# Weight loads ahead of later steps' loads on SP, and results written from ScalarE's queue

## The chip, the core and the metric

One NeuronCore of a Trainium2 chip runs the whole program. The metric is the device time of one execution in microseconds (us); the median over the runs is taken. The profile adds one execution with its hardware trace.

## What is computed

Attention over four batches of 8 heads, 768 positions and head size 64. Each query sees the first four keys (the sinks) and a window of the last 128. What attention gives, 3072 rows of 512, goes through a two-layer network with 2048 hidden units. Inputs and results are float32.

```python
def _attn_ref(q, k, v, n_sink, window):
    scores = scale * np.matmul(q, k.transpose(0, 1, 3, 2))
    is_sink = pos[None, :] < int(n_sink)
    rel = pos[:, None] - pos[None, :]
    keep = is_sink | ((rel >= 0) & (rel < int(window)))
    scores = np.where(keep, scores, -1000000000.0)
    ...
    return np.matmul(a, v).astype(np.float32)

def _moe_ref(x, w_in, w_out):
    h = x @ w_in
    sp = np.maximum(h, 0.0) + np.log1p(np.exp(-np.abs(h)))
    g = h * erf(sp)
    return (g @ w_out).astype(np.float32)
```

`w_in` and `w_out` arrive as float64.

## The kernel before, in words

**Work.** The 3072 rows are cut into 12 groups of 256. A group has four attention steps, one for each pair of heads, so there are 48 steps (0 to 47). Each step loads k and q (tile `kq`) and v (tile `v`), turns them (`tqk`), multiplies (`ps`), takes the softmax on VectorE (DVE) and ScalarE (ACT), turns the weights of the softmax (`tp`, `ts` in the first steps, through `turn`, `pd`, `pa` in DRAM later) and multiplies with v (`av`). The network follows behind: for each group 16 slices of the hidden layer (`h`, lines L766 and L770), the function on ACT (L783 to L788, three `u` tiles for each pair of slices) with its products on DVE (L792), giving `gf` in the first part and `g` (L799 on DVE, L800 on GpSimd) later, then the second product into `o` (L812, later L815 to L817), then a copy `ot` (L821, ACT) and a DMA to the result (L732). Each group has two results, `ot_g_0` and `ot_g_1`, so there are 24.

**Weights.** They come in 32 blocks of 512 KB (`ws`, L653). Three DVE instructions for a block (L665, L670, L673) make float32 of float64's two halves (`wf`). While not all are there, TensorE (PE) multiplies in float32 straight from `wf` (L766, L812: the float32 stage); later ACT and DVE split them (`wt`, L684, L685) and PE runs on the split form (L770, L815 to L817). `wl` issues the next blocks, up to ten ahead of those converted.

**Sinks.** The first four rows of v are needed for each step. For later groups they are spread into a DRAM tile `sinks` once (`set_sinks`, L253): one DMA of 1024 KB from `vz` (L256) and four of 64 KB from the input (L263). From step 12 on, a group's steps read them back (L248).

**Order.** The Tile framework's scheduler writes out each engine's order from priorities: `with at(a, what)` gives the place of what is issued there, `plan` says which step does what at which place. `follow(prev, ins)` (L330) only says that `ins` stands behind `prev` in that order; nothing waits on it. SP issues nearly all DMAs, one after another. A DMA that is issued waits on its engine for its data, for its buffer, and on one of eight semaphores (`DMAHW0` to `DMAHW7`) for the landing of an earlier DMA, the one issued eight before it as a rule. Results share their buffers (tag `u`, four of them) with the `u` tiles.

The lines that the change touches: L225 and L241 (kq and v in `load`, L209), L256 in `set_sinks`, L653 in `wload`, L732. Numbers behind names (`ws_394`, `gf_713`) count tiles as they are made; `kq_890` and `v_932` are those of step 8, `v_1090` of step 9, `v_1221` of step 10, and `ws_186` is the ninth weight block.

Of the kernel before, what the change touches and what calls it, by code (L numbers as in the profile page):

```python
# [9 lines left out]
F32 = mybir.dt.float32  # L10
BF16 = mybir.dt.bfloat16
F32R = mybir.dt.float32r
I32 = mybir.dt.int32
# [6 lines left out]
P = 128  # L20
# [42 lines left out]
def kernel(  # L63
# [11 lines left out]
    nc = tc.nc  # L75
    B, H, S, D = q.shape
    NT, DM = out.shape
# [60 lines left out]
    def fast_path():  # L138
        with ExitStack() as st:
# [20 lines left out]
                out=kw[:, :256], in0=rf[:, :256], scalar=0.0, in1=kw[:, :256], op0=ALU.is_ge, op1=ALU.mult  # L160
# [42 lines left out]
            mark = {}  # L203
# [5 lines left out]
            def load(s, what="kq"):  # L209
                g, c = divmod(s, NPAIR)  # L210
                b, gb = divmod(g, GPB)
                d = stp.setdefault(s, {})
                if "k" in what:
                    t = d["kq"] = raw.tile([P, 2, GT], F32, tag="kq", bufs=1, name=f"kq_{s}")
                    if s < DT:
                        d["k"], d["q"] = (t[:, j].rearrange("p (n h d) -> p n h d", n=2, h=2) for j in range(2))
                if "k" in what or "q" in what:
                    t = d["kq"]
                    last = mark.get(("d", s - 2))
                    for j, src in enumerate((k, q)):  # L220
                        if "kq"[j] not in what:
                            continue
                        for h in range(2):
                            if s < DT:
                                nc.sync.dma_start(  # L225
                                    d["kq"[j]][:, :, h, :],
                                    src[b, 2 * c + h, gb * GT : (gb + 1) * GT, :].rearrange("(n p) d -> p n d", p=P),
                                )
                                continue
                            for e in range(2):  # L230
                                p0 = 64 * h + 32 * e
                                x = nc.sync.dma_start(
                                    t[p0 : p0 + 32, j, :].rearrange("p (n c) -> p n c", c=32),
                                    src[b, 2 * c + h, gb * GT : (gb + 1) * GT, 32 * e : 32 * e + 32].rearrange("(n r) c -> r n c", r=32),
                                )
                                last = mark["l", s] = follow(last, x)
                if "v" in what:
                    t = d["v"] = raw.tile([P, 3, 2, D], F32, tag="v", bufs=1 + AL, name=f"v_{s}")
                    m0 = 0 if gb == 0 else 1
                    for h in range(2):  # L240
                        x = nc.sync.dma_start(  # L241
                            t[:, 1 - m0 :, h, :],
                            v[b, 2 * c + h, gb * GT - m0 * P : (gb + 1) * GT, :].rearrange("(n p) d -> p n d", p=P),
                        )
                        follow(mark.get(("r", s - 2), mark.get(("l", s))), x)
                if gb == 0 and "v" in what:
                    for z, hf in enumerate((hi, lo)):
                        nc.sync.dma_start(  # L248
                            vz[hf, z, :, 2 * c : 2 * c + 2].rearrange("p i h d -> p i (h d)"),
                            sinks[b * NPAIR + c].rearrange("p i h d -> p i (h d)"),  # L250
                        )

            def set_sinks():  # L253

                x = vz[HP : HP + 2 * SW, 0, 1].rearrange("p h d -> p (h d)").rearrange("p (o f) -> p o f", o=1)
                nc.sync.dma_start(  # L256
                    sinks.rearrange("n p i h d -> (n p i h d)").rearrange("(p o f) -> p o f", p=2 * SW, f=H * D),
                    x.broadcast_to([2 * SW, B * NPAIR, H * D]),
                )
                for i in range(2):  # L260
                    for h in range(2):
                        r0 = 2 * SW * i + SW * h
                        nc.sync.dma_start(  # L263
                            sinks[:, r0 : r0 + SW, i, h],
                            v.rearrange("b (c h) s d -> h (b c) s d", h=2)[h, :, :SW, :],
                        )
# [63 lines left out]
            def follow(prev, ins):  # L330

                if prev is not None:
                    tc.add_manual_dep(
                        ins.ins, prev.ins.name,
                        mybir.DependencyInfo(mybir.DependencyClass.NoSync, mybir.DependencyReason.DATA), reason="order",
                    )
                return ins
# [246 lines left out]
            def at(a, what):  # L584

                key = int(a * PW) + O[what] + (E.get(what, 0) if a < EA else 0)
                return tc.high_priority(offset=tc.tile_snap_priority() + 1 - key)

            def pos(s):

                return s if s < NE else 3 * s - 6 if s < 2 * NPAIR else 4 * s - 12

            plan = {}
            for s in range(NSTEP + AL):
# [23 lines left out]
                if s < 2 * NPAIR:  # L618
                    x = pos(s) + (3 if s < NE else 5)
# [9 lines left out]
            def attn(a):  # L629

                for what, fn, s in sorted(plan.get(a, ()), key=lambda x: (STAGES.index(x[0]), x[2])):
                    with at(a, "prepl" if what == "prep" and s > TT else what):
                        fn(s)
# [3 lines left out]
            def need(n):  # L637
                return 4 * (n // 4) if n < 16 else n - 16 + LAG
# [3 lines left out]
            for n in range(32):  # L642
                x = n - 16
                split.setdefault(NF - 5 + n if x < 0 else NF + 6 + (x - FH) * 5 // 4 if x >= FH else 2 * NF - 1 + x * 2 // 3, []).append(n)

            def wload(n):

                src = wblock(n)
                t = staged[n] = wpool.tile([P, 2 * DM], I32, tag="wo", name=f"ws_{n}")
                if src.dtype == F32:  # L650
                    nc.sync.dma_start(t[:, :DM].bitcast(F32), src)
                else:
                    nc.sync.dma_start(t, src.bitcast(I32))  # L653

            def wconv(n, wn):

# [30 lines left out]
            def wblock(n):  # L687
                if n < 16:
                    j, c = divmod(n, NC)
                    return w_in[c * P : (c + 1) * P, WB * j : WB * j + WB]  # L690
                return w_out[(n - 16) * P : (n - 15) * P, :]

            mlp = make_mlp(work, ps_h, ps_o)
# [18 lines left out]
            for m in range(-LEAD, NG * NF + LAG + 2):  # L712
                a = m + LEAD
                live = 0 <= m < NG * NF
                if live:
                    g, f = divmod(m, NF)
                    if f % 2 == 0:
                        hp = mlp.hid_tile(m)
                    if f > 0:
                        with at(a, "hid"):  # L720
                            ahead = mlp.hidden(hp, xp[g], f)
                attn(a)
                w = m - LAG
                if 0 <= w < NG * NF:
                    g2, f2 = divmod(w, NF)
                    with at(a, "proj"):
                        mlp.project(gs[w // 2], g2, f2, lambda ins: follow(ahead if live and f and g >= 2 else None, ins))
                    if f2 == NF - 1:
                        for i in range(2):
                            r0 = (g2 * 2 + i) * P  # L730
                            with at(a, "res"):
                                nc.sync.dma_start(out[r0 : r0 + P, :], mlp.result(g2, i))  # L732
                if live:
                    if f == 0:
                        with at(a, "hid"):
                            mlp.hidden(hp, xp[g], f)
                    if f % 2 == 1:
                        with at(a, "act"):
                            gs[m // 2] = mlp.act(hp, m, m < NF + FH)

                while wn < 32 and a >= 1 and (wn < (0, 0, 3, 5)[a - 1] if a < 5 else wn < 2 * a - 4 or need(order[wn]) <= m + W1):
                    with at(a, "wc"):
                        wconv(order[wn], wn)
                    wn += 1
                    with at(a, "wl"):
                        for n in order[wl : wn + WQ]:
                            wload(n)
                            wl += 1
                for n in split.get(m, ()):
                    with at(a, "ws"):  # L750
                        wsplit(n, m)
# [72 lines left out]
    def general_path():  # L824

        NT_S = S // P
        with ExitStack() as st:
# [71 lines left out]
            with tc.tile_pool(name="g_one1", bufs=1) as one, tc.tile_pool(name="g_work1", bufs=2) as work:  # L899
# [3 lines left out]
                with tc.For_i(0, B, 1) as b:  # L903
                    for gb in range(GPB):
# [25 lines left out]
                        for i in range(2):  # L930
# [3 lines left out]
                            )  # L934

    fast_path()
    ok = nc.values_load(flagi[0:1, 0:1], min_val=0, max_val=1)
    with tc.If(ok == 0):
# [31 lines left out]
```

## Time and profile before

| what | before |
|---|---|
| median of 3 runs | 718.12 us (716.73 to 719.35) |
| the profiled execution | 719.41 us |
| its span in the trace | 717.4 us |
| mean granted clock of PE | 0.993 |
| busy: PE, DVE, ACT, GpSimd (POOL) | 96%, 77%, 69%, 42% |

The span is what the trace covers; 2.0 us of the profiled execution lie outside it. Busy times are shares of the span; the clock is the share of full speed that was granted to PE.

### The profile page before, as it was taken

How to read it: one execution, taken by the hardware profiler on the slowest of the kernel's cores; microseconds unless marked ns; L12 is line 12 of the kernel's file. 1: busy time of each engine (PE TensorE's matmuls, PEld its weight loads, DVE VectorE, ACT ScalarE, POOL GpSimd, SP SyncE). 2: the span in 40 equal slices, each digit the busy share in tenths (PEclk: the TensorE clock that was granted, in tenths of full speed). 3: DMA queues.
4: the chain of work that ended last, by engine and by line, in shares of the span. 5: the costliest groups of instructions: out<-in, count | busy, mean ns of one | idle time of the engine just before them, and what ended most of it. 6: DMA issues, size and time to landing. Idle time of an engine off the chain costs nothing. (4 is left out here: it accounts for less than half of the span.)

```text
span 717.4 us, 16155 instructions
## 1 busy us (share of the span) xinstructions
PE 689.5 (96%) x5515; PEld 568.2 (79%) x5515; DVE 549.4 (77%) x1473; ACT 493.6 (69%) x1157; POOL 299.1 (42%) x501
## 2 busy tenths in 40 slices
PE   6779999999999999999999999999999999999997
PEld 3566557688887888788788888888888888889885
DVE  6979997687789888788888588688698687754352
ACT  4777676986984867476677586586677577586572
POOL 3412400234444546454554444555554437342221
PEclk9999999999999999999999999999999999999999
DMA  6999410302216454543553363463463543220001
GB/s 159 283 320 344 168 27 5 78 16 46 66 34 118 102 117 100 127 104 72 124 118 72 65 135 74 87 136 75 95 124 72 102 96 71 44 68 1 30 1 35
DMA packets 246858, 70.10 MB, mean 98 GB/s; under 512 B 214704, under 2 KB 238896, under 8 KB 246768
## 3 DMA queue, kind: packets, MB, share of 16 engines
q1 hardware_dynamic: 246208, 68.92, 41.1%
q8 instruction: 46, 0.75, 0.4%
q14 instruction: 44, 0.36, 0.2%
q10 hardware_dynamic: 560, 0.07, 0.1%
HBM read 50.27 MB, written 18.42 MB: 96 GB/s over the span
## 5 line engine op out<-in xcount | busy, mean ns | idle before, releaser
L770 PE MATMUL h<-xh,wt 128*128 128x256 f32 x1408 | 275.1, 284 | 0.8 <-DVE u L792 0.7
L770 PEld LDWEIGHTS h<-xh,wt 128*128 128x128 f32 x1408 | 223.7, 188 | 15.4 <-issue 8.2
L770 PE MATMUL h<-xl,wt 128*128 128x256 f32 x704 | 197.3, 281 | 0.0
L800 POOL TENSOR_TENSOR g<-u,g 128x512 fp32r<-128x512 f32 x84 | 113.9, 1356 | 181.3 <-DVE g L799 160.1
L788 ACT ACTIVATE u<-r 128x512 f32<-128x512 f32 x288 | 163.1, 622 | 19.2 <-DMA out_dram<-ot 5.3
L792 DVE SCALAR_TENSOR_TENSOR u<-u,u 128x512 f32<-128x512 f32 x168 | 136.6, 813 | 14.0 <-ACT u L788 1.6
L770 PEld LDWEIGHTS h<-xl,wt 128*128 128x128 f32 x704 | 132.1, 188 | 7.0 <-issue 2.8
L815 PE MATMUL o<-wt,g 128*128 128x512 f32 x336 | 134.1, 399 | 0.5 <-DVE g L799 0.5
L816 PE MATMUL o<-wt,g 128*128 128x512 f32 x336 | 132.8, 395 | 0.0
L817 PE MATMUL o<-wt,g 128*128 128x512 f32 x336 | 129.8, 397 | 0.6 <-POOL g L800 0.4
L426 ACT ACTIVATE pst<-pst,neg 128x144 f32<-128x144 f32 x192 | 77.4, 405 | 61.0 <-DVE neg L422 60.7
L792 DVE SCALAR_TENSOR_TENSOR u<-u,h 128x512 f32<-128x512 f32 x84 | 56.8, 676 | 54.9 <-ACT u L788 53.1
L783 ACT ACTIVATE r<-h 128x512 f32<-128x512 f32 x96 | 56.8, 592 | 51.0 <-PE h L770 42.8
L522 POOL TENSOR_SCALAR_AFFINE_SELECT pz<-pa 64x256 f32<-64x256 f32 (+1 forms) x96 | 47.1, 491 | 70.0 <-ACT pa L484 68.9
L815 PEld LDWEIGHTS o<-wt,g 128*128 128x128 f32 x336 | 63.0, 187 | 14.6 <-ACT u L788 1.3
L817 PEld LDWEIGHTS o<-wt,g 128*128 128x128 f32 x336 | 61.7, 187 | 16.0 <-POOL g L800 1.4
L816 PEld LDWEIGHTS o<-wt,g 128*128 128x128 f32 x336 | 63.0, 188 | 10.8 <-issue 0.3
L785 ACT ACTIVATE r<-r 128x512 f32<-128x512 f32 x96 | 60.6, 631 | 2.8
L784 ACT ACTIVATE r<-r 128x512 f32<-128x512 f32 x96 | 60.6, 631 | 2.6
L799 DVE CAST g<-u 128x512 fp32r<-128x512 f32 x84 | 37.4, 445 | 27.3 <-PE o L817 24.1
L513 POOL COPY pz<-pa 64x256 f32<-64x256 f32 x66 | 31.5, 477 | 55.4 <-DMA pa<-pd 54.6
L522 POOL TENSOR_SCALAR_AFFINE_SELECT pa<-pa 64x256 f32<-64x256 f32 (+1 forms) x96 | 50.4, 525 | 4.9
(99 smaller groups left out, 916.6 us busy)
## 6 DMA issues: line engine op xcount, KB each, us to landing
pd<-turn SPq DMA_DIRECT2D x33, 320.0 KB, 2.6
pa<-pd SPq DMA_DIRECT2D x132, 80.0 KB, 2.6
ws<-in_moe_w_in_dram SPq DMA_DIRECT2D x16, 512.0 KB, 6.1
ws<-in_moe_w_out_dram SPq DMA_DIRECT2D x16, 512.0 KB, 8.5
out_dram<-ot SPq DMA_DIRECT2D x24, 256.0 KB, 2.4
v<-in_v_dram SPq DMA_DIRECT2D x56, 96.0 KB, 2.5
kq<-in_k_dram SPq DMA_DIRECT2D x144, 32.0 KB, 2.0
kq<-in_q_dram SPq DMA_DIRECT2D x144, 32.0 KB, 2.2
```

The source lines that it names most:

```text
L426: mark["e", s] = nc.scalar.activation(y, y, AF.Exp, bias=d["neg"][:, i, h : h + 1], scale=-1.0, accum_out=d["sum"][:, i, h : h + 1])
L522: nc.gpsimd.affine_select(out=out, in_=x, pattern=[[0, 2], [0, 2 - i0], [-sg, HP]], compare_op=op, fill=0.0, base=0, channel_multiplier=sg,)
L770: last = nc.tensor.matmul(o, wt[NC * j + c][:, p, fs], xt[e][:, c, :], start=(m == 0), stop=(m == len(ops) - 1))
L783: nc.scalar.activation(r, h, AF.Tanh, bias=b_t, scale=0.5)
L784: nc.scalar.activation(r, r, AF.Square, bias=b_v, scale=-0.5)
L785: nc.scalar.activation(r, r, AF.Square, bias=b_r)
L788: sq = nc.scalar.activation(u, r, AF.Square, bias=b_a[i], scale=CS)
L792: pr = nc.vector.scalar_tensor_tensor(out=acc, in0=u, scalar=CC[i] * CS**2, in1=x, op0=ALU.add, op1=ALU.mult)
L800: nc.gpsimd.tensor_tensor(gl, acc, gh.bitcast(F32), op=ALU.subtract)
L815: behind(nc.tensor.matmul(o, gh[:, ws], wt[16 + f][:, 0, :], start=(f == 0), stop=False))
L816: nc.tensor.matmul(o, gh[:, ws], wt[16 + f][:, 1, :], start=False, stop=False)
L817: nc.tensor.matmul(o, gl[:, ws], wt[16 + f][:, 0, :], start=False, stop=(f == NF - 1))
```

## The change

kq and v loads of steps that are issued once a weight DMA is on record, and the sinks' spreading, are put behind the last weight DMA that is on record at that point of the program. Results are issued on ACT's queue.

```diff
@@ load @@
-                                nc.sync.dma_start(
+                                x = nc.sync.dma_start(
...
+                                follow(mark["w"], x)
...
-                        follow(mark.get(("r", s - 2), mark.get(("l", s))), x)
+                        follow(mark.get(("r", s - 2), mark.get(("l", s), mark["w"])), x)
@@ set_sinks @@
-                nc.sync.dma_start(
+                x = nc.sync.dma_start(
                     sinks.rearrange("n p i h d -> (n p i h d)").rearrange("(p o f) -> p o f", p=2 * SW, f=H * D),
                     x.broadcast_to([2 * SW, B * NPAIR, H * D]),
                 )
+                follow(mark["w"], x)
@@ wload @@
-                    nc.sync.dma_start(t, src.bitcast(I32))
+                    mark["w"] = nc.sync.dma_start(t, src.bitcast(I32))
@@ results @@
-                                nc.sync.dma_start(out[r0 : r0 + P, :], mlp.result(g2, i))
+                                nc.scalar.dma_start(out[r0 : r0 + P, :], mlp.result(g2, i))
```

Line numbers of the changed kernel are up to two higher. Three places of the order that it sets:

**SP behind the ninth weight block.** Before, with `ws_394` the tenth block:

```order
L653 DMA ws_186<-in_moe_w_out_dram 128x1024
L937 TENSOR_LOAD flagi
L937 ISA x2
L241 DMA v_932<-in_v_dram 128x3x64 x2
L241 DMA v_1090<-in_v_dram 128x3x64 x2
L256 DMA sinks<-vz 512x1x512
L653 DMA ws_394<-in_moe_w_out_dram 128x1024
L653 DMA ws_396<-in_moe_w_out_dram 128x1024
L653 DMA ws_401<-in_moe_w_out_dram 128x1024
L241 DMA v_1221<-in_v_dram 128x3x64 x2
```

The same queue in the changed kernel, from the last weight block on (`ws_814`):

```order
L655 DMA ws_814<-in_moe_w_out_dram 128x1024
L225 DMA kq_890<-in_k_dram 128x2x64 x2
L225 DMA kq_890<-in_q_dram 128x2x64 x2
L242 DMA v_932<-in_v_dram 128x3x64 x2
L242 DMA v_1090<-in_v_dram 128x3x64 x2
L257 DMA sinks<-vz 512x1x512
L242 DMA v_1221<-in_v_dram 128x3x64 x2
L265 DMA sinks<-in_v_dram 16x16x64 x4
```

The v loads of steps 8 to 10, the kq loads of step 8 and the five DMAs of the spreading stood between weight blocks, and now stand behind all of them.

**DVE at the tenth weight block.** Before, from the last work ahead of it to the first product of `gf_713`:

```order
L665 TENSOR_SCALAR wf_579<-ws_186 128x512
L673 SCALAR_TENSOR_TENSOR wf_558<-ws_181,wf_558 128x512
L670 SCALAR_TENSOR_TENSOR wf_579<-ws_186,wf_579 128x512
L433 TENSOR_SCALAR sum_537<-sum_537 128x4
L673 SCALAR_TENSOR_TENSOR wf_579<-ws_186,wf_579 128x512
L434 RECIPROCAL sum_537<-sum_537 128x4
L456 TENSOR_TENSOR snk_576<-pst,sum_537 128x128
L665 TENSOR_SCALAR wf_579<-ws_394 128x512
L670 SCALAR_TENSOR_TENSOR wf_579<-ws_394,wf_579 128x512
L417 COPY_PREDICATED ps_622<-tri,ps_622 64x2x2x64
L792 SCALAR_TENSOR_TENSOR gf_713<-u_1_717,h_652 128x512
```

Changed, from that block's first conversion (which now stands two instructions behind `ws_186`'s) on:

```order
L667 TENSOR_SCALAR wf_579<-ws_394 128x512
L672 SCALAR_TENSOR_TENSOR wf_579<-ws_186,wf_579 128x512
L435 TENSOR_SCALAR sum_537<-sum_537 128x4
L672 SCALAR_TENSOR_TENSOR wf_579<-ws_394,wf_579 128x512
L675 SCALAR_TENSOR_TENSOR wf_579<-ws_186,wf_579 128x512
L667 TENSOR_SCALAR wf_609<-ws_396 128x512
L436 RECIPROCAL sum_537<-sum_537 128x4
L675 SCALAR_TENSOR_TENSOR wf_579<-ws_394,wf_579 128x512
L667 TENSOR_SCALAR wf_609<-ws_401 128x512
L672 SCALAR_TENSOR_TENSOR wf_609<-ws_396,wf_609 128x512
L458 TENSOR_TENSOR snk_576<-pst,sum_537 128x128
L794 SCALAR_TENSOR_TENSOR gf_713<-u_1_717,h_652 128x512
```

The conversions of the tenth block, and half of those of the two after it, moved ahead of the softmax's `snk_576` and of `gf_713`.

**ACT at the results of group 5**, with what each instruction waits for. Before:

```order
L821 COPY ot_0_5200<-o_0_4502 128x512 [waits PE_49]
L821 COPY ot_1_5203<-o_1_4503 128x512 [waits PE_49]
L788 ACTIVATE u_99_5210<-r_5206 128x512 [waits Activation_49,Pool_49]
L788 ACTIVATE u_99_5213<-r_5206 128x512 [waits Pool_49]
L581 CAST xh_5169<-av_5488 128x256 [waits PE_49]
L788 ACTIVATE u_99_5216<-r_5206 128x512 [waits DMAHW5_49,Activation_49]
```

Changed:

```order
L823 COPY ot_0_5200<-o_0_4502 128x512 [waits PE_49,Pool_49]
L734 DMA out_dram<-ot_0_5200 128x512 [waits DMAHW7_49,Activation_49]
L823 COPY ot_1_5203<-o_1_4503 128x512 [waits PE_49]
L790 ACTIVATE u_99_5210<-r_5206 128x512
L790 ACTIVATE u_99_5213<-r_5206 128x512 [waits Pool_49]
L583 CAST xh_5169<-av_5488 128x256 [waits PE_49]
L734 DMA out_dram<-ot_1_5203 128x512 [waits DMAHW2_49,Activation_49]
L790 ACTIVATE u_99_5216<-r_5206 128x512 [waits DMAHW7_49]
```

Each result's DMA now stands in ACT's order, and waits there for an earlier DMA's landing as well as for its copy. At the first of them `DMAHW7` stands for the landing of the first q load of step 33, which SP issues; at the last `u` it stands for the first result's own landing.

## Rows read from the trace of the kernel before

**Rows 1.** The page's first part: busy us, share of the span, instructions.
```profile
PE 689.5 (96%) x5515; PEld 568.2 (79%) x5515; DVE 549.4 (77%) x1473; ACT 493.6 (69%) x1157; POOL 299.1 (42%) x501
```

**Rows 2.** Waits of PE: total us, times, longest us.
```profile
PE av L563 <- POOL pa L522: 6.5, 5, 2.8
```

**Rows 3.** Stretches: us; busy PE, PEld, DVE, ACT, POOL; PEclk, DMA share, GB/s.
```profile
36.00:54.00 18.00, 14.06 (x97) 10.67 (x97) 13.45 (x40) 13.66 (x38) 3.01 (x6) 0.91 1.01 320
48.00:53.00 5.00, 5.00 (x16) 3.95 (x15) 4.91 (x16) 3.84 (x12) 1.34 (x2) 0.66 1.04 406
54.00:72.00 18.00, 18.00 (x107) 12.10 (x104) 17.84 (x46) 12.75 (x33) 5.21 (x6) 1.00 1.04 344
72.00:90.00 18.00, 16.82 (x110) 10.72 (x108) 17.91 (x42) 12.17 (x31) 8.76 (x13) 1.00 0.41 163
97.00:126.00 29.00, 29.00 (x174) 18.83 (x173) 23.95 (x64) 18.16 (x45) 1.66 (x4) 1.00 0.05 10
```

**Rows 4.** Timeline of PE: start us, us, what [idle before <-releaser].
```profile
47.84 5.38 PE L766 MATMUL h<-xf,wf 128*128 128x256 f32 x16 [3.47 <-DVE gf L792]
...
57.60 3.62 PE L766 MATMUL h<-xf,wf 128*128 128x256 f32 x16
...
85.75 0.70 PE L766 MATMUL h<-xf,wf 128*128 128x256 f32 x2 [0.87 <-DVE wf L673]
86.68 2.43 PE L766 MATMUL h<-xf,wf 128*128 128x256 f32 x10 [0.24 <-DVE wf L673]
```

**Rows 5.** Timeline of DVE around the tenth weight block.
```profile
38.44 0.42 DVE L665 TENSOR_SCALAR wf<-ws 128x512 int32<-128x512 int32 x1
...
45.50 0.43 DVE L665 TENSOR_SCALAR wf<-ws 128x512 int32<-128x512 int32 x1 [4.29 <-DMA ws<-in_moe_w_out_dram]
...
47.02 0.67 DVE L792 SCALAR_TENSOR_TENSOR gf<-u,h 128x512 f32<-128x512 f32 x1
```

**Rows 6.** Timeline of SP: DMAs issued behind the ninth weight block, and the last weights.
```profile
34.53 1.99 SPq L241 DMA_DIRECT2D v<-in_v_dram  x4
36.56 0.70 SPq L256 DMA_DIRECT2D sinks<-vz  x1
37.31 4.93 SPq L653 DMA_DIRECT2D ws<-in_moe_w_out_dram  x3
...
64.20 5.94 SPq L653 DMA_DIRECT2D ws<-in_moe_w_out_dram  x8
```

**Rows 7.** DMAs issued from 30 to 92 us: KB each, us to landing.
```profile
sinks<-vz SPq DMA_DIRECT2D x1, 1024.0 KB, 7.5
```

**Rows 8.** Waits of SP on the results' copies: total us, times, longest us.
```profile
SPq L732 <- ACT ot L821: 108.5, 10, 41.3
```

**Rows 9.** ACT's timeline at the start: one of three DMAs that it issues.
```profile
1.28 0.45 ACTq L293 DMA_DIRECT2D q_early<-in_q_dram  x1
```

**Rows 10.** ACT's timeline at the results of group 5.
```profile
410.84 1.29 ACT L821 COPY ot<-o 128x512 f32<-128x512 f32 x2 [0.72 <-PE o L817]
...
413.94 0.63 ACT L788 ACTIVATE u<-r 128x512 f32<-128x512 f32 x1 [0.50 <-DMA out_dram<-ot]
```

**Rows 11.** SP's timeline there.
```profile
413.36 2.33 SPq L232 DMA_DIRECT2D kq<-in_q_dram  x4
```

**Rows 12.** The page's last part, DMA issues: KB each, median us to landing.
```profile
out_dram<-ot SPq DMA_DIRECT2D x24, 256.0 KB, 2.4
...
kq<-in_q_dram SPq DMA_DIRECT2D x144, 32.0 KB, 2.2
```

**Rows 13.** DVE's timeline there: the cast of that step's product.
```profile
416.05 0.43 DVE L799 CAST g<-u 128x512 fp32r<-128x512 f32 x1
```

**Rows 14.** PE's timeline there: the first matmul that reads it.
```profile
419.15 0.40 PE L815 MATMUL o<-wt,g 128*128 128x512 f32 x1
```

**Rows 15.** ACT's timeline at the end: the last two copies.
```profile
711.73 1.23 ACT L821 COPY ot<-o 128x512 f32<-128x512 f32 x2 [4.81 <-PE o L817]
```

More of the change, by code (lines that the diff above doesn't have):

```diff
@@ L650, in wload @@
                 if src.dtype == F32:
-                    nc.sync.dma_start(t[:, :DM].bitcast(F32), src)
+                    mark["w"] = nc.sync.dma_start(t[:, :DM].bitcast(F32), src)
                 else:
-                    nc.sync.dma_start(t, src.bitcast(I32))
+                    mark["w"] = nc.sync.dma_start(t, src.bitcast(I32))
             def wconv(n, wn):
```

## The prediction

> **What bounds the kernel now.** I began with the page's busy times: TensorE works 96% of the span [rows 1], so the end moves only by what PE loses in idle time or at a lower clock. PE's list of waits names no large one that repeats; the longest kind is for GpSimd's `pa`, 6.5 us in five waits of at most 2.8 [rows 2]. So the question is which single losses the change touches, and the stretches tell where to look. From 36 to 54 us PE is busy 14.06 of 18 us, at 0.91 of the clock, while DMA is at 1.01 of its engines [rows 3]. Here the loads are the limit. From 54 to 90 us DVE is busy 17.84 and 17.91 of 18 [rows 3]: there the conversion of weights is the limit. After that neither is full: from 97 to 126 us PE is busy 29.00 of 29, DVE 23.95, DMA at 0.05.
>
> The timelines name the loss. DVE stands 4.29 us until 45.50 for the tenth weight block [rows 5]. Behind that conversion stands the first product of `gf` at 47.02, and PE stands 3.47 us for it, until 47.84 [rows 4, 5]. Then PE is slower still: sixteen matmuls take 5.38 us where the same sixteen take 3.62 at 57.60 [rows 4], and the granted clock from 48 to 53 us is 0.66 on average [rows 3], so part of it ran at 1.2 GHz in place of 2.4 after the idle time. Two more waits, 0.87 and 0.24 us, are for conversions at 85.75 and 86.68 [rows 4].
>
> **Part one: the loads.** Before the tenth block SP issues four v loads and the 1024 KB spreading [rows 6]. They hold 4 times 96 KB and 1024 KB, 1.41 MB; at the 320 GB/s of that stretch [rows 3] that is 4.4 us, and the spreading alone needs 7.5 us from issue to landing [rows 7]. Without them in front the tenth block lands at least 4.4 us earlier than 45.50, at 41.1 or before, and DVE has work until then: its last instruction before the wait ends 4.29 us ahead of 45.50, at 41.2. So I take the whole wait as gone. The later blocks gain more, since the v of step 10, the kq of step 8 and the four small spreading loads leave too; DMA stays ahead of DVE, which needs about 1.7 us for a block (0.43 for L665 [rows 5], some 0.6 for each of the other two, an estimate from the spacing of rows in that timeline).
>
> What does PE get? Its losses in this stretch are 3.47 of idle time, 5.38 less 3.62, which is 1.76, of clock, and 0.87 with 0.24, which is 1.11, of later waits: 6.34 in all [rows 4]. But DVE is full from 54 to 90 us, and PE waits for its conversions again near 86, so up to there PE cannot come further ahead than DVE does: 4.29. The bounds are 2.4 (3.47 of idle time without the clock, and 1.11 of waits for conversions once more) and 6.3. I take **4.3**, since the full rows of DVE make that the limit. The clock comes back in this as part of the 4.3: without the 3.47 us of idle time before it I expect full speed in those sixteen matmuls.
>
> The moved loads get late themselves. The last weights are issued from 64.20 to 70.1 [rows 6]; the change lets them end earlier and puts kq of step 8, v of steps 8 to 10 and the spreading behind. In the changed order PE turns step 8's kq behind more of the float32 stage's products than before, so nothing waits where it waited before. What is later on PE is the attention of steps 7 and 8, in the stretch from 97 to 126 us; PE has no idle time there and DVE has 5 of 29 us free [rows 3]. Price: **0**, at most 2.8, the longest wait that PE has for the attention's other parts [rows 2], and not below zero, as PE is full there.
>
> **Part two: the results.** 24 DMAs leave SP for ACT. ACT's own issues at the start take 0.45 us [rows 9], so 24 of them are 10.8 us of ACT, which is busy 69% [rows 1]; PE does not wait for ACT in most places, so this alone costs nothing. Its cover is ACT's free 31%; where that is gone the waits are priced next. SP loses the waits for the copies, 108.5 us in ten [rows 8]; no wait of PE is laid to SP's results, so I count no gain.
>
> The new cost is that a result's DMA waits on ACT for an earlier DMA's landing, with the `u` activations behind it. At group 5 the two copies run 410.84 to 412.13, so the first ends near 411.43 [rows 10]. In the order that the change sets, its DMA waits for the first q load of step 33, which SP issues at 413.36 [rows 11] and which lands 2.2 us later [rows 12], 415.6. Without results SP comes there a little sooner, say 415.4. ACT stands about 4 us. The result lands 2.4 us after its issue [rows 12], at 417.8, and the third `u`, which waits for that landing, starts then and not at 413.94 [rows 10]: 3.9 us later. The cast of that step's product moves from an end of 416.48 [rows 13] to 420.4, and PE wants it at 419.15 [rows 14]. PE loses **1.2**; between 0 (if SP's queue comes early enough) and 3.9 (if nothing else can run). At the other groups the semaphore's DMA is mostly landed when the copy ends, and I take 0.
>
> *A rule weighed.* The row of SP's waits shows that SP issues nothing while a result waits for its copy: 108.5 us in ten waits [rows 8]. The Trainium skill, page "Perfetto Trace Analysis", section "DMA Instruction — HWDGE (DVE, Sync)", says that the issuing sequencer itself sits in the semaphore wait before a DMA, and that the profiled time starts only behind it. By that rule ACT stands behind the waiting DMA as SP does, and 1.2 us are lost at group 5; were activations let past it, the loss would be 0 and the predicted time 1.2 us less. The trace has no waiting DMA on ACT to show which.
>
> The end: both last copies run back to back, 1.23 us from 711.73 [rows 15]. Now the first result's issue, 0.45 us [rows 9], stands between them, and the last result is late by that. Cost **0.45**.
>
> **Sum**, on the profiled execution: 719.41 - 4.3 + 0 + 1.2 + 0.45 = 716.8. The profiled execution lies 1.29 above the median of the three runs, so against 718.12 the 2.65 us make **715.5**. A difference under 0.3% (2.15 us) can't be told from no change here.
>
> **Rivals.**
> - *ACT's queue becomes the bound (slower).* If landings are late at more results than group 5's, each such group costs PE about 1.2 us. It decides at four groups: 4 times 1.2 is 4.8, more than the 3.85 that are left (4.3 less 0.45). With five it is 6.0, and the time 718.12 - 3.85 + 6.0 = 720.3. For it: in the changed order 22 of the 24 results wait for another landing, and a `u` behind them. Against it: SP reached ten results before their copies [rows 8], so its earlier DMAs were long issued. Chance 0.14.
> - *Given back later (no change that can be told).* The attention that moved behind the float32 stage leaves PE waiting for kq or softmax between 97 and 126 us, for half of the 2.8 bound. Then 718.12 - 2.65 + 1.4 = 716.9. For it: DVE and ACT get that work later, and step 9's kq is loaded only when step 8's is turned. Against it: PE's full 29.00 us there [rows 3]. Chance 0.34.
> - *All of PE's loss comes back.* If the changed order gives PE work that needs no conversion, DVE's lead is no cap: 6.3, and group 5 finds its landing early: 718.12 - 6.3 + 0.45 = 712.3. Against it: DVE's 17.84 and 17.91 of 18. Chance 0.12.
>
> **How the numbers follow.** My forecast, 715.5, has 0.40. With the third rival, faster has 0.52; same 0.34; slower 0.14. The range from 712.8 to 719.2 takes in the forecast's unknown costs on the later side (2.8 for late steps) and most of the two milder rivals; it leaves out most of the slower one and the edge of the best one.
>
> **What would show it.** Right: no DVE wait for a weight block after 40 us; PE's sixteen matmuls behind that place in about 3.6 us and the granted clock from 36 to 54 near 1.00; the stretch to 90 us ends some 4 us earlier for the same work; one ACT idle time of about 4 us at group 5's first result, and PE waiting there for DVE's `g` about a microsecond. Wrong: PE waits for `tqk` or `tp` after 90 us that add up to more than 2 us; ACT idle ahead of results at several groups, with PE waits for `g` behind them; or a new DVE wait for weights.

## The result and the profile after

| | before | after |
|---|---|---|
| median of 13 runs, us | 718.79 (716.73 to 722.63) | 724.62 (722.67 to 729.61) |
| ratio, 95% interval | | 1.0087 (1.0062 to 1.0113) |
| profiled execution, us (span) | 719.41 (717.4) | 725.74 (723.7) |

The changed kernel is slower by 0.87%, 5.8 us, where 715.5 was forecast. The 13 runs of after lie in two groups by the mean granted clock of the run: eight at 0.989 or more took 722.67 to 725.74 us, five at 0.984 to 0.987 took 726.71 to 729.61; the profiled one is of the first group.

The page's first part of after, to be read against [rows 1]:

```profile
PE 693.1 (96%) x5515; PEld 569.7 (79%) x5515; DVE 552.0 (76%) x1473; ACT 493.0 (68%) x1157; POOL 297.2 (41%) x501
```

The same instructions in the same numbers, and PE is busy 3.6 us longer. The stretches of after (columns as in [rows 3]) tell where:

```profile
36.00:54.00 18.00, 15.78 (x94) 11.25 (x93) 17.38 (x47) 15.24 (x40) 3.07 (x6) 1.00 1.01 333
...
54.00:72.00 18.00, 18.00 (x114) 11.58 (x113) 17.88 (x42) 11.95 (x31) 4.75 (x6) 1.00 1.03 368
72.00:90.00 18.00, 17.16 (x92) 11.94 (x91) 17.88 (x44) 10.62 (x31) 7.58 (x8) 1.00 0.52 110
...
97.00:126.00 29.00, 25.03 (x167) 15.68 (x162) 16.91 (x51) 13.76 (x38) 5.21 (x10) 0.99 0.12 28
126.00:132.00 6.00, 5.98 (x28) 4.80 (x28) 2.59 (x4) 5.87 (x13) 1.95 (x4) 0.76 0.24 90
```

From 36 to 54 us PE gains 1.7 us of busy time and the whole clock. From 97 to 126, where it had been full [rows 3], PE now stands idle for 4 of 29 us, and behind that the clock is granted at 0.76.

**Where the loads were.** DVE's timeline of after at the tenth weight block and at the first product of `gf`, then PE's at the places of [rows 4]:

```profile
38.88 0.43 DVE L667 TENSOR_SCALAR wf<-ws 128x512 int32<-128x512 int32 x1 [0.32 <-DMA ws<-in_moe_w_out_dram]
...
43.47 0.68 DVE L794 SCALAR_TENSOR_TENSOR gf<-u,h 128x512 f32<-128x512 f32 x1
```

```profile
44.88 3.62 PE L768 MATMUL h<-xf,wf 128*128 128x256 f32 x16
49.53 3.70 PE L814 MATMUL o<-wf,gf 128*128 128x512 f32 x8 [0.81 <-DVE gf L794]
...
84.58 1.98 PE L814 MATMUL o<-wf,gf 128*128 128x512 f32 x4 [0.59 <-DVE wf L675]
```

DVE's 4.29 us [rows 5] are 0.32 now. The sixteen matmuls take 3.62 us, as at full clock, with no idle time ahead. So much came as forecast. To say how far PE is ahead I take the work that PE has begun by a given time in each of the two kernels (each matmul counted at the median time from its start to the next matmul's, for its kind in before). By this count after is 3.4 us ahead of before at 90 us.

**Where the time went.** PE's timeline of after behind that:

```profile
96.45 0.67 PE L565 MATMUL av<-pa,v_early 128*64 128x64 f32 x12 [0.73 <-ACT pa L486]
...
98.19 0.66 PE L353 MATMUL tqk<-ident,kq 128*128 128x128 f32 x4 [0.60 <-ACT pz L490]
...
101.24 0.39 PE L772 MATMUL h<-xh,wt 128*128 128x256 f32 x1 [1.10 <-DVE gf L794]
...
103.02 0.56 PE L406 MATMUL ps<-kq 64*64 64x208 f32 x2
103.51 0.33 PE L565 MATMUL av<-pa,v_early 128*64 128x64 f32 x2
...
124.47 0.89 PE L480 MATMUL tp<-ident,pst 128*128 128x128 f32 x4 [1.62 <-DVE pst L443]
...
126.02 0.58 PE L772 MATMUL h<-xh,wt 128*128 128x256 f32 x1 [0.47 <-DVE gf L794]
126.40 0.41 PE L772 MATMUL h<-xl,wt 128*128 128x256 f32 x1
...
129.31 0.28 PE L772 MATMUL h<-xl,wt 128*128 128x256 f32 x1
```

And PE's timeline of before where it does the same work:

```profile
89.04 0.67 PE L563 MATMUL av<-pa,v_early 128*64 128x64 f32 x12
...
90.11 0.65 PE L351 MATMUL tqk<-ident,kq 128*128 128x128 f32 x4
90.60 3.62 PE L766 MATMUL h<-xf,wf 128*128 128x256 f32 x16
94.06 3.60 PE L812 MATMUL o<-wf,gf 128*128 128x512 f32 x8
97.58 0.56 PE L404 MATMUL ps<-kq 64*64 64x208 f32 x2
```

In before, step 6's `av` (89.04) and the turning of step 8's kq (90.11) stand ahead of 24 float32 matmuls, 7.0 us of work (90.60 to 97.58) that needs nothing of these steps' attention. In after such products run first, from 86.40 to 96, and the attention comes when they are used up: PE stands idle for 0.73, 0.60, 0.21 and 1.10 us up to 101.24, then for 1.62 and 0.47 at 124 to 126, and behind that, up to 129, its matmuls run at half clock (0.41 us at 126.40, 0.28 at 129.31). The waits are 4.7 us: 3.2 for parts of the attention, 1.6 (1.10 and 0.47) for `gf` of the network. The clock is 1.4 (0.24 of 6 us). By the count above PE goes from 3.4 us ahead at 90 us to 4.0 behind at 130, 7.5 us; waits and clock make 6.2 of them (4.73 and 1.44), the rest is scattered.

DVE had no free time there. These are stretches of after, then of before:

```profile
96.00:102.00 6.00, 3.64 (x45) 3.14 (x46) 6.00 (x10) 5.00 (x11) 4.16 (x6) 1.00 0.19 43
```

```profile
96.00:102.00 6.00, 6.00 (x26) 2.46 (x24) 6.00 (x12) 4.62 (x9) 0.00 (x0) 1.00 0.00 0
102.00:108.00 6.00, 6.00 (x36) 3.32 (x35) 5.91 (x12) 2.52 (x5) 0.00 (x0) 1.00 0.20 46
```

DVE is busy 6.00 of 6 us from 96 to 102 in both kernels, and 5.91 up to 108 in before. The 5 of 29 us that it had free from 97 to 126 [rows 3] lie behind that.

The data was not late. SP's timeline of after:

```profile
53.93 9.20 SPq L655 DMA_DIRECT2D ws<-in_moe_w_out_dram  x8
64.13 1.54 SPq L225 DMA_DIRECT2D kq<-in_k_dram  x2
...
73.52 0.68 SPq L257 DMA_DIRECT2D sinks<-vz  x1
```

Step 8's kq is issued at 64 and turned at 98.19, and that turning waits for ACT's `pz`. Between 78 and 131 us the trace of after has no wait of any engine for a DMA.

**The results.** ACT's timeline of after, at groups 3 and 5 and at the end, then PE's at group 3:

```profile
306.94 0.40 ACTq L734 DMA_DIRECT2D out_dram<-ot  x1
307.39 0.41 ACT L428 ACTIVATE pst<-pst,neg 128x144 f32<-128x144 f32 x1 [2.58 <-DMA pa<-pd]
...
307.81 0.56 ACT L823 COPY ot<-o 128x512 f32<-128x512 f32 x1
...
417.63 0.35 ACTq L734 DMA_DIRECT2D out_dram<-ot  x1
...
420.34 0.64 ACT L790 ACTIVATE u<-r 128x512 f32<-128x512 f32 x1 [0.42 <-DMA out_dram<-ot]
...
718.30 0.59 ACT L823 COPY ot<-o 128x512 f32<-128x512 f32 x1 [0.46 <-PE o L819]
718.92 0.34 ACTq L734 DMA_DIRECT2D out_dram<-ot  x1
```

```profile
308.42 0.50 PE L817 MATMUL o<-wt,g 128*128 128x512 f32 x1 [1.90 <-ACT ot L823]
```

At group 5 ACT waits 0.42 us, not 4. The stand that was priced there is at group 3: the result's DMA waits for a landing of `pa` and is issued only at 306.94; in the 2.58 us up to 307.39 ACT runs nothing, and the second copy, which stands behind, is late for PE by 1.90 us. That ACT runs nothing that is queued behind a waiting DMA agrees with the Trainium skill, page "Perfetto Trace Analysis", section "DMA Instruction — HWDGE (DVE, Sync)": the sequencer sits in the wait.

At the end the last copies stand 0.46 us apart, for which 0.45 was priced. But the end of the span moved by more than that. PE's last matmul, in before and in after:

```profile
711.94 0.40 PE L817 MATMUL o<-wt,g 128*128 128x512 f32 x1
```

```profile
717.47 0.40 PE L819 MATMUL o<-wt,g 128*128 128x512 f32 x1
```

From its end the span goes on for 5.1 us in before (712.34 to 717.4) and for 5.8 in after (717.87 to 723.7). The last result lands no later behind that matmul, by its issue and landing: 3.3 us in before (issued at 712.99, 2.6 to landing) and 3.2 in after (718.92 and 2.2). What comes later is the end of the program behind the landing.

### The profile page after: what moved, and what is told of

It is laid out like the page before. It is cut to its first block, busy times and chain, and to the rows that moved or that the text cites. A ratio compares the mean times of both kernels' runs of the same rounds, so it can differ in the third digit from the quotient of the medians.

```text
span 723.7 us, 16166 instructions
## 1 busy us (share of the span) xinstructions
PE 693.1 (96%) x5515; PEld 569.7 (79%) x5515; DVE 552.0 (76%) x1473; ACT 493.0 (68%) x1157; POOL 297.2 (41%) x501
## 5 line engine op out<-in xcount | busy, mean ns | idle before, releaser
L772 PE MATMUL h<-xh,wt 128*128 128x256 f32 x1408 | 278.9, 286 | 2.4 <-DVE gf L794 1.6
L772 PEld LDWEIGHTS h<-xh,wt 128*128 128x128 f32 x1408 | 226.3, 190 | 19.0 <-issue 8.6
L772 PEld LDWEIGHTS h<-xl,wt 128*128 128x128 f32 x704 | 133.6, 190 | 6.2 <-issue 2.1
L406 PE MATMUL ps<-kq 64*64 64x208 f32 (+2 forms) x768 | 52.3, 362 | 0.5 <-ACT kq L360 0.5
```

Source lines behind the costliest of these rows:

```text
L406: nc.tensor.matmul(ps[h][hf, x : x + n], qt[r, hf], kt[r, r0 : r0 + n], start=True, stop=True),
L772: last = nc.tensor.matmul(o, wt[NC * j + c][:, p, fs], xt[e][:, c, :], start=(m == 0), stop=(m == len(ops) - 1))
```

## The experiments

My theory after the result: the moved loads make the scheduler write another order on all engines, and it is the order that costs. The rivals: late data of steps 8 to 10, and ACT's queue. Each kernel was timed beside before on the same chip; the medians of before in the four batches are 719.34, 719.20, 719.09 and 718.96 us.

**The two parts apart.** `loads` is after with the results on SP, `results` is before with them on ACT:

```
loads:    nc.sync.dma_start(out[r0 : r0 + P, :], mlp.result(g2, i))
results:  nc.scalar.dma_start(out[r0 : r0 + P, :], mlp.result(g2, i))
```

> The loads' part alone; results are issued by SP as before. Theory A (order): the loads change the order in which PE gets the float32 stage and the attention of steps 7 to 10, and PE starves between 96 and 130 us; then most of the loss is here: 3 to 6 us slower than before, some 722 to 725, with the four PE waits at 96 to 102 us and those at 124 to 126 again. Theory B (results): the loss is ScalarE standing on landings; then this part alone has the gain of the first 90 us and is about 3 us faster than before, 715 to 716.

> The results' part alone; loads in the order of before. Theory A: little, 0 to 2.5 us slower (718.8 to 721), the most at group 3, where PE waits for the second copy behind ScalarE's wait for pa. Theory B: 5 us slower or more (724).

`loads` took 725.01 us (1.0080, 1.0052 to 1.0108), `results` 720.96 (1.0022, 1.0006 to 1.0038). So the loads' part alone makes a loss as large as the whole change's, and the results alone cost 1.6 us; the two don't add up. The stretches of `loads`, and a row of its PE timeline:

```profile
102.00:108.00 6.00, 6.00 (x20) 2.48 (x18) 2.37 (x4) 0.60 (x2) 0.00 (x0) 0.54 0.01 3
108.00:114.00 6.00, 6.00 (x31) 3.29 (x30) 1.57 (x4) 0.37 (x1) 0.00 (x0) 0.50 0.00 0
```

```profile
103.08 0.95 PE L406 MATMUL ps<-kq 64*64 64x208 f32 x2
```

The same waits as in after stand at 96 to 101 us, and here the work behind them runs at half clock: step 8's scores and step 7's `av`, which take turns two matmuls at a time. The pair at 103.08 takes 0.95 us, in after 0.56. With these turns at half clock the profiled execution of `loads` (729.74 us, where its median is 725.01) lies 4.3 us above after's in span.

**One load at a time.** Of the three `follow(mark["w"], x)`, `sinks` keeps that of the sinks' spreading alone, `kqonly` that of step 8's kq, `vs` those of v and of the spreading; results on SP:

```
sinks:   x = nc.sync.dma_start(sinks...); follow(mark["w"], x)
kqonly:  x = nc.sync.dma_start(d["kq"[j]]...); follow(mark["w"], x)
vs:      follow(mark.get(("r", s - 2), mark.get(("l", s), mark["w"])), x)   and as sinks
```

> Only the sinks' spreading is put behind the last weight block; v, kq and the results as before. The spreading held the weights up by some 5 us, so VectorE's wait for the tenth block should be under 1 us. Theory A: the order of PE changes less than in loads, but changes; 715 to 720. If what was lost came from kq and v being late, this should be 3 us faster than before.

> Only step 8's kq loads are put behind the last weight block. The order of PE is that of before, instruction for instruction, so this has the late data without the changed order. Theory A (order): no change to 1 us faster, 718 to 719.5. Theory C (the moved loads come late): slower by 2 us or more, with PE waiting for step 8's tqk.

> The v loads and the spreading behind the last weight block, kq where it was. PE, ACT, DVE and GpSimd have the order of the run loads, instruction for instruction; only step 8's kq lands early. Theory A (order): the loss of loads stays, 723 to 726. Theory C (late data): 2 us or more faster than loads.

`kqonly`: 719.37 us (1.0005, 0.9986 to 1.0025), with PE's order that of before. A kq that comes behind all weights shows no cost. `vs` leaves kq early, has the order of `loads` on all engines but SP, and is slow: 728.09 (1.0107, 1.0068 to 1.0146), again with the turns at half clock (granted 0.56 and 0.50 from 102 to 108 and to 114 us). So it is not late kq. Late v has no run of its own; `pin` and `loadsni`, further down, have all loads as late as `loads` and don't lose. `sinks`: 717.40 (0.9981, 0.9966 to 0.9995), faster by 1.9. A row of its DVE timeline:

```profile
40.53 0.43 DVE L666 TENSOR_SCALAR wf<-ws 128x512 int32<-128x512 int32 x1 [1.08 <-DMA ws<-in_moe_w_out_dram]
```

Moving the spreading alone takes DVE's wait from 4.29 to 1.08 us. Its order differs from before's too: there step 7's `av` and step 8's scores hardly take turns.

**The order put back.** `pin` is `loads` with two rows of PE's order held by `follow`, which nothing waits on: the float32 first products of slice 14 stand behind step 8's turning, the second products of slices 10 and 11 behind step 9's:

```
+ mark["tq", s] = nc.tensor.transpose(...)
...
+ ahead = mlp.hidden(hp, xp[g], f, lambda ins: follow(mark["tq", 8] if m == 14 else None, ins))
...
+ mlp.project(gs[w // 2], g2, f2, lambda ins: follow(mark["tq", 9] if w == 10 else ..., ins))
```

> The loads' part alone as in the run loads, and two order dependencies on PE that wait for nothing: the hidden layer's slice 14 stands behind step 8's tqk, and the second products of slices 10 and 11 behind step 9's tqk, as they did before. The loads land as late as in loads. Theory A: PE's waits between 96 and 130 us go, and the gain of the first 90 us stays: 714.5 to 717. Theory C (the moved loads are late themselves): the time stays within 1 us of the run loads, with PE waiting for tqk's loads instead.

719.21 us (1.0004, 0.9985 to 1.0023): 5.8 less than `loads`, with the same loads. So the order makes the loss. But the 714.5 to 717 that were expected are missed: this order doesn't bring the gain either. A stretch of `pin`:

```profile
90.00:96.00 6.00, 4.66 (x37) 4.04 (x38) 6.00 (x11) 5.94 (x14) 3.66 (x6) 0.53 0.01 2
```

Its float32 stage ends early as well, and what is early meets the attention not ready: PE waits for `pst`, `snk` and `pa`, 2.9 us from 87 to 92 us, and runs at half clock behind.

**The turns taken away.** One more `follow` puts step 8's scores behind all of step 7's `av`, so that the two don't take turns. `noilv` is before with it, `loadsni`, `pinni` and `afterni` are `loads`, `pin` and after with it, `sinkspinni` is `sinks` with it and with the two of `pin`:

```
  def av(s):
      ...
+     mark["av", s] = prev
...
  prev = mark.get(("p", s - 1)) if s - AL == 3 * NPAIR - 1 else mark["av", 7] if s == 8 else None
```

> The loads and the results of before; one order dependency puts step 8's scores behind step 7's av, which PE ran two and two by turns before (6.7 us in the trace of before, where each of the two alone takes about 1 us). If the turns cost time, 3 to 5 us faster, 714 to 716; if the time between is work or wait of another kind, no change. This is also the reference for the next run, whose order has no turns either.

> The loads' part with the two order dependencies of the run pin, and step 8's scores behind step 7's av. If turns cost time on a clock that has fallen, as pin's trace suggests (half clock from 90 to 97 us), 4 to 6 us faster than pin: 713.5 to 715.5. If they cost nothing: 719, as pin.

> The loads' part, its order as in loads, but step 8's scores behind step 7's av. If half of the loss is the stretch of turns on a clock that has fallen (14 us at half clock from 102 to 116 us in the trace of loads), 4 to 7 us faster than loads: 718 to 721, with the PE waits at 96 to 102 us still there. If the turns cost only what they cost in noilv (2.2 us): 722.8.

> The whole changed kernel, results on ScalarE too, with one order dependency: step 8's scores behind step 7's av. If the two parts add (loadsni 715.1, results 1.6 more): 716 to 718, faster than before by 1 to 3 us and some 7 us faster than the changed kernel; the waits for step 7's softmax at 96 to 102 us stay, the wait and the fallen clock at 124 to 129 us go. If the results' queue is what makes the loss in the whole kernel: 721 or more.

> Only the spreading behind the last weight block, the order dependencies of pinni, results by SP. Theory A: the gain of VectorE's wait and of the turns without the loss of order: 713.5 to 716.5, as fast as pinni or faster, since v lands early and the waits for step 7's softmax at 88 to 93 us of pinni's trace go.

| kernel | median, us | ratio to before | against the same without it, us |
|---|---|---|---|
| `noilv` | 716.99 | 0.9962 (0.9948 to 0.9975) | -2.2 |
| `pinni` | 715.86 | 0.9945 (0.9926 to 0.9964) | -3.4 |
| `loadsni` | 715.09 | 0.9937 (0.9915 to 0.9960) | -9.9 |
| `afterni` | 714.31 | 0.9939 (0.9921 to 0.9957) | -10.3 |
| `sinkspinni` | 713.29 | 0.9909 (0.9883 to 0.9934) | |

`noilv` gained less than the 3 to 5 us that were expected, `loadsni` and `afterni` more than was expected of them. Where the turns are gone there is a block of each. PE's timeline of `afterni`:

```profile
101.52 0.67 PE L565 MATMUL av<-pa,v_early 128*64 128x64 f32 x12
102.02 0.64 PE L565 MATMUL av<-pz,vz 128*64 128x64 f32 x16
102.59 0.99 PE L406 MATMUL ps<-kq 64*64 64x208 f32 x16
```

That is 2.0 us from start to start of what follows, where before's turns go from 97.58 to 104.25, 6.7 us. The stretches of `loadsni`:

```profile
96.00:102.00 6.00, 4.11 (x45) 3.57 (x43) 6.00 (x10) 5.02 (x11) 3.90 (x6) 0.87 0.19 44
102.00:108.00 6.00, 6.00 (x62) 4.33 (x61) 5.12 (x11) 1.08 (x3) 0.00 (x0) 0.84 0.01 3
...
126.00:132.00 6.00, 6.00 (x81) 5.44 (x80) 3.84 (x7) 5.91 (x13) 2.03 (x4) 1.00 0.16 38
```

The waits at 96 to 101 us are there as in `loads` (PE busy 4.11 of 6 us), but half clock ends by about 104, and there is no wait at 124 to 130. `afterni` has after's order on PE up to the turns, and so the same waits ahead of them, 0.72, 0.60, 0.21 and 1.08 us; of these in PE's timeline:

```profile
95.73 0.67 PE L565 MATMUL av<-pa,v_early 128*64 128x64 f32 x12 [0.72 <-ACT pa L486]
...
100.50 0.38 PE L773 MATMUL h<-xh,wt 128*128 128x256 f32 x1 [1.08 <-DVE gf L795]
```

So 2.6 us of after's waits belong to the products that were pulled forward. The waits at 124 to 126 and the half clock behind them, 3.5 us, are gone without the turns. From the turns on the order of `afterni` differs from after's in more than this row, since the scheduler moves others with it; which of them matters is not shown. With loads and results moved as in after, `afterni` keeps the forecast's gain and more: 4.6 us below before in its batch. Against `noilv`, which has the turns away and no load moved, it is 2.7 us below by the medians, 1.7 by the ratios (0.9939 and 0.9962, whose intervals just overlap); so much, if anything, both parts of the change are worth in an order that doesn't spoil them. `sinkspinni` has the lowest median here, 5.8 us below before in its batch; its interval overlaps with those of the three rows above it.

**A late order without late loads.** `late` has before's loads and results, but step 8's turning of kq stands behind the second products of slice 11, and no turns came of it:

```
+ mlp.project(gs[w // 2], g2, f2, (lambda ins: follow(ins, mark["tq", 8])) if g2 == 0 else ...)
```

> The loads and the results of before; one order dependency puts step 8's tqk behind the second products of slices 10 and 11, as the changed kernel has it. No load is moved. The turns of scores and av go with it, so it is compared with noilv. Theory A: 3 us or more slower than noilv, with PE waits for the attention between 96 and 130 us. If the order is not the cause: within 1 us of noilv.

724.31 us (1.0059, 1.0038 to 1.0080). With all loads in their old places an order alone costs 7.3 us against `noilv`. But its losses are not where after has them. From PE's waits in `late`:

```profile
PE tp L480 <- DVE pst L443: 4.1, 3, 2.7
PE ps L406 <- POOL kq L360: 2.0, 1, 2.0
```

The long ones (2.72, 1.04 and 1.96 us) lie at 167 to 180 us, not at 96 to 130 as expected. So this shows that an order can cost as much, and doesn't copy after's mechanism.

**Group 3's results on SP.** `results3` is `results` with these two left on SP:

```
(nc.sync if g2 == 3 else nc.scalar).dma_start(out[r0 : r0 + P, :], mlp.result(g2, i))
```

> As the run results, but group 3's two results stay on SP. If the 1.6 us that the results' part costs are ScalarE's stand at group 3, 718.8 to 719.8 and no wait of PE for ot there; if they are spread over the groups, 720.5 to 721.5.

720.31 us (1.0023, 1.0005 to 1.0040), the same ratio as `results`. PE's idle time for `ot` at group 3 (1.64 us in `results`) is gone, and another has come, in PE's timeline of `results3`:

```profile
310.65 0.50 PE L815 MATMUL o<-wt,g 128*128 128x512 f32 x1 [1.77 <-DVE g L799]
```

So ACT's stand at group 3 is not what the results' part costs in all. In the profiled executions some 0.6 us of it are at the end: from the last matmul to the end of the span it is 5.7 us in `results` and 5.6 in `results3`, against 5.1 in before. Where the rest goes stays open.

## Why the prediction was wrong

- **The loads' gain: right.** DVE's 4.29 us went to 0.32, the sixteen matmuls to 3.62 us, the clock from 36 to 54 to 1.00, and PE was 3.4 us ahead at 90 us for a forecast of 4.3. The cap that I took from DVE's full stretch held: 17.88 of 18 from 54 to 72 and from 72 to 90.
- **"Price: 0, at most 2.8", the late steps: this step failed.** I saw in the changed order that step 8's kq is turned behind more float32 products, and read from it that "nothing waits where it waited before". I read the stretch from 97 to 126 us [rows 3], with PE at 29.00 of 29 us and 5 us of DVE free, as one with room for the rest; but DVE had no free time in it before 102, and hardly any before 108. PE was full because float32 products stood between the parts of the attention. Pulled forward they were gone, and PE waited there 4.7 us and lost 1.4 of clock. The 3.4 us gained and 4.0 more were given back between 90 and 130 us. That the order does it and not the data is shown by `kqonly` (late kq, old order: no change), `vs` (early kq, new order: slow), `pin` (late loads, part of the old order: 5.8 us less) and `loadsni` (late loads, one more `follow`: 9.9 less, where the same `follow` takes 2.2 from before). What each row of the order costs is shown only in part: the products ahead cost 2.6 us of waits, which `afterni` has too, and it is faster than before; the other losses need the turns behind these waits. Why those turns are at half clock in one execution and at full clock in another is open.
- **The rival "given back later"** named the place, and with the softmax the cause of most of the waits; the 1.6 us for `gf` it did not name. It was sized at 1.4 us, half of a single wait of before; it needed several waits and the clock behind each, 7.5 us. The longest wait of before was no bound for an order that before doesn't have.
- **Group 5's 1.2 us:** no stand there. The mechanism, ACT standing behind a result that waits for a landing, came at group 3, and cost PE 1.90 us there. `results` sizes the whole part at 1.6 us (0.0022 of 719.3), what I had summed for it (1.2 and 0.45). That the two agree is luck: `results3` says that the sum is made up in another way. In after the ACT queue did not become the bound, as that rival had it: `loads` without it is as slow.
- **The tail, 0.45:** the copies are 0.46 us apart as priced, though an issue on ACT takes 0.34 us (the median of 24; 0.45 was taken). That the last result is late by it was wrong: it lands 3.2 us behind the last matmul, as before. The end of the span behind that matmul is 0.8 us later in after and 0.6 in `results`.

## What to carry to other kernels

Where a scheduler orders all engines, a moved DMA changes the order of matmuls as well, and that can weigh more than the wait it removes: read the new order around every place where long independent work stood between dependent steps, and ask what fills them now. A full stretch of PE doesn't show that there is room for more, and the free time of another engine, taken over a long stretch, doesn't show when it is free. Then hold the order that matters with dependences that nothing waits on, as `sinkspinni` does, and time a kernel whose loads alone, and one whose order alone, is changed.

## What the runs showed of the hardware

- **These matmuls are dear in turns.** Sixteen score matmuls (64x64 weights) and 28 of `av`, two and two in turns, take 6.7 us at granted clock 1.00 (before, 97.58 to 104.25); as blocks, 2.0 us (`afterni`). Not all of it came back in time: taking the turns from before gained 2.2 us. What it is in the two kinds that makes their turns slow is not shown.
- **PE without idle time at half clock.** In `loads` PE was busy 6.00 of 6 us in the turns from 102 to 108 and from 108 to 114, and the clock was granted at 0.54 and 0.50, the 1.2 GHz level, to the end of the turns; the waits up to 101.08 us stood before them. It came back in the float32 products that follow. In `loadsni`, with blocks in their place, the same waits cost half clock up to about 104 only. In after the turns ran at 0.56 us a pair, full clock, behind the same waits; what decides between the two is open.
